# Column norms by one 512-column product with ones as weights, in place of four one-column products

## The chip, the cores and the metric

The kernel runs on one core of one Trainium2 chip. The time is that of one execution on the device, in microseconds (us); it is given as the median of several runs. The profile is of one such execution, and has its own span.

## The reference

Four batches of 6400 rows and 256 columns. Each column of q and of k is divided by its norm over the 6400 rows; the 256 x 256 product of kn and qn goes through a softmax along its rows; v is multiplied by it; and each row of the result gets the sum of two low-rank adapters, chosen by a gate, added.

```python
def _attn_ref(q, k, v, tau):                      # 4 x 6400 x 256
    qn = q / (np.linalg.norm(q, axis=1, keepdims=True) + 1e-06)
    kn = k / (np.linalg.norm(k, axis=1, keepdims=True) + 1e-06)
    s = kn.transpose(0, 2, 1) @ qn / tau
    s = s - s.max(-1, keepdims=True)
    a = np.exp(s)
    a /= a.sum(-1, keepdims=True) + 1e-09
    return (v @ a).astype(np.float32)

# x = that, as 25600 rows; 8 experts, rank 16, the 2 largest of 8 logits
    logits = x @ w_gate
    ...
            z = x[mask] @ A[e]
            delta[mask] += w[mask, k, None] * (z @ B[e])
    return (x + delta).astype(np.float32)
```

## The kernel before

A batch is cut into 50 chunks of 128 rows. Loads convert from float32 to bfloat16 on the way and come in tiles of 10 chunks: `qk` tiles hold q and k side by side (four buffers), `vt` tiles hold v (five buffers). They are issued by GpSimd (POOL) from one list in the order in which they will be needed, each as soon as its buffer is free (`load_more`).

The statistics of a batch come from three things for each chunk. `square` (line 164) squares two chunks of q and k at once, on ScalarE, or in batch 0 in turn on VectorE and ScalarE. `gram` (line 176) adds k-transposed times q to `acc`, two products of 256 moving columns. `norm` (line 187) adds up the squares over the rows: the squares are the weights, 128 columns of them at a time, and a single column of ones is moved through, so that a chunk takes four products with one moving column each, and the 4 x 128 sums stand in four columns of the tile `nrm`, one column of q or k to a partition.

After the last chunk the batch goes through a chain of stages, `chain0` to `chain6`:

- `chain0`: square roots of the four columns of sums, as Ln and Exp on ScalarE (lines 204 and 206).
- `chain1`: the small constant is added and the reciprocal taken (212, 214) on VectorE; the reciprocals of q's norms are laid on the diagonal of `dg` (217); ScalarE multiplies `acc` by the reciprocals of k's norms, which are one to a partition, into `tk` (221).
- `chain2`: a float32 product of ones and `dg` broadcasts q's reciprocals to all partitions, in the other half of `nrm` (228), and VectorE multiplies `tk` by that into `s_sb` (231).
- `chain3` to `chain6`: the exponential `ae` with its row sums (239), its transposes (251), the products with the gate's and the adapters' weights (267, 269), and the scaled matrices `wa_sb` and `a_bf`.

`acc` and `nrm` have one buffer each, so a batch's first Gram product and first norm product reuse the banks of the batch before.

For batch 0 all of this runs first, in order: chunks by twos, norms four chunks behind, then its chain without anything between. Then a loop of slots begins (lines 517 to 565), 100 of them for the 100 pairs of chunks of v. In each slot TensorE transposes one pair (316), computes z (422), transposes the gated z (446), and adds up y from v (438) and the adapters (458); every fifth slot it computes the logits of a group of five pairs (337). VectorE gates z (426), copies transposes (327, 452) and works through the gating operations of the last group (360 to 405), dealt out a few to a slot by `deal`, in the order of a credit; ScalarE copies y to `ys` (462). Woven into the slots are the chunks of the next batch, by the table `GRAM`: batch 1 in slots 0 to 20, batch 2 in 24 to 45, batch 3 in 49 to 67. The stages of a chain take a slot each after that: those of batch 1 start in slot 21, those of batch 2 in 46, those of batch 3 in 68. The second number of a stage in `CHAIN` is taken off the credit of its slot. `chain0` to `chain3` are issued at the start of their slot, ahead of the slot's Gram products; `chain4` to `chain6` at its end.

Outputs go out in groups of five pairs. Up to six finished groups are held back until slot 67 and released step by step after it (`send`).

The order on each engine is the program's order: the schedule is manual.

Of the kernel before, what the change touches and what calls it, by code (L numbers as in the profile page):

```python
# [8 lines left out]
FP32 = mybir.dt.float32  # L9
BF16 = mybir.dt.bfloat16  # L10
AX = mybir.AxisListType
OP = mybir.AluOpType
ACT = mybir.ActivationFunctionType
# [3 lines left out]
def kernel(  # L17
# [16 lines left out]
    nc = tc.nc  # L34
    B, N, C = q.shape
    P = 128
    NC = N // P
    CC = C // P
# [21 lines left out]
    const = ctx.enter_context(tc.tile_pool(name="const", bufs=1))  # L60
# [5 lines left out]
    bat = ctx.enter_context(tc.tile_pool(name="bat", bufs=2))  # L66
# [40 lines left out]
    def load_more(limit=1000):  # L107

        while limit and at_load[0] < len(loads):
            _, kind, b, s, parts = loads[at_load[0]]  # L110
            n = len(left[kind])
            if n >= bufs[kind] and left[kind][n - bufs[kind]]:
                return
            where[kind, b, s] = n
            left[kind].append(PC)
            c0 = s * PC
            if kind == "qk":
                t = qk_pool.tile([P, 2, PC, C], BF16, tag="qk", name="qk")
            else:
                t = v_pool.tile([P, PC, C], BF16, tag="v", name="vt")  # L120
            tiles[kind][b, s] = t
            o = 0
            for m in parts:
                if kind == "qk":
                    nc.gpsimd.dma_start(t[:, 0, o:o + m, :], q_v[b, :, c0 + o:c0 + o + m, :])  # L125
                    nc.gpsimd.dma_start(t[:, 1, o:o + m, :], k_v[b, :, c0 + o:c0 + o + m, :])
                else:
                    nc.gpsimd.dma_start(t[:, o:o + m, :], v_v[b, :, c0 + o:c0 + o + m, :])  # L128
                o += m
            at_load[0] += 1  # L130
            limit -= 1
# [10 lines left out]
    make_identity(nc, ident)  # L142
    ident_f = const.tile([P, P], FP32)
    make_identity(nc, ident_f)
    ones_bf = const.tile([P, 2], BF16)
    nc.vector.memset(ones_bf, 1.0)
    ones_f = const.tile([P, P], FP32)
    nc.vector.memset(ones_f, 1.0)
    neg_inv_tau = const.tile([P, 1], FP32)
    nc.vector.memset(neg_inv_tau, -inv_tau)  # L150
    load_more(3)
# [10 lines left out]
    acc, nrm, sqs = {}, {}, {}  # L162

    def square(b, c, eng):

        s, o = divmod(c, PC)
        t = tiles["qk"][b, s]
        sq = sq_pool.tile([P, 2, 2, C], BF16, tag="sq", name="sq")
        sqs[b, c] = sq
        src = t[:, :, o:o + 2, :]  # L170
        if eng == "act":
            nc.scalar.activation(sq, src, ACT.Square)  # L172
        else:
            nc.vector.tensor_tensor(out=sq, in0=src, in1=src, op=OP.mult)  # L174
# [12 lines left out]
    def norm(b, c):  # L187
        if c == 0:
            nrm[b] = ps_nrm.tile([P, 512], FP32, tag="nrm", name="nrm")
        sq = sqs[b, c - c % 2]  # L190
        for w in range(2):
            for ic in range(CC):
                j = w * CC + ic
                nc.tensor.matmul(  # L194
                    nrm[b][:, j:j + 1], sq[:, w, c % 2, ic * P:(ic + 1) * P], ones_bf[:, 0:1],
                    start=(c == 0 and j == 0), stop=(c == NC - 1), skip_group_check=True)


    st = {}

    def chain0(b):
        d = st.setdefault(b, {})
        lnn = bat.tile([P, 4], FP32, name="lnn")
        nc.scalar.activation(lnn, nrm[b][:, 0:4], ACT.Ln)
        rt = bat.tile([P, 4], FP32, name="rt")
        nc.scalar.activation(rt, lnn, ACT.Exp, scale=0.5)
        d["rt"] = rt

    def chain1(b):
        d = st[b]  # L210
        rt = d["rt"]
        nc.vector.tensor_scalar(out=rt, in0=rt, scalar1=1e-6, scalar2=None, op0=OP.add)
        rr = bat.tile([P, 4], FP32, name="rr")
        nc.vector.reciprocal(rr, rt)
        dg = bat.tile([P, CC, P], FP32, name="dg")
        for ic in range(CC):
            nc.vector.tensor_scalar(out=dg[:, ic, :], in0=ident_f, scalar1=rr[:, ic:ic + 1],
                                    scalar2=None, op0=OP.mult)
        tk = bat.tile([P, CC, C], FP32, name="tk")
        for ic in range(CC):  # L220
            nc.scalar.activation(tk[:, ic, :], acc[b][:, ic, :], ACT.Copy,
                                 scale=rr[:, CC + ic:CC + ic + 1])
        d["dg"], d["tk"] = dg, tk

    def chain2(b):
        d = st[b]
        bc = nrm[b][:, 256:512]
        nc.tensor.matmul(bc, ones_f, d["dg"].rearrange("p c d -> p (c d)"), start=True, stop=True)
        s_sb = bat.tile([P, CC, C], FP32, name="s_sb")
        for ic in range(CC):  # L230
            nc.vector.tensor_tensor(out=s_sb[:, ic, :], in0=bc, in1=d["tk"][:, ic, :], op=OP.mult)
        d["s"] = s_sb

    def chain3(b):
# [44 lines left out]
    def chain6(b):  # L279
        d = st[b]  # L280
        a_bf = bat.tile([P, CC, C], BF16, name="a_bf")
        for ic in range(CC):
# [2 lines left out]
        d["a"] = a_bf  # L285


    CHAIN = [(chain0, 0.0), (chain1, 0.9), (chain2, 0.75), (chain3, 0.0), (chain4, 0.55),
             (chain5, 0.65), (chain6, 0.5)]


    groups = []
    for b in range(B):
        f = 0
# [117 lines left out]
    def z_gz(u):  # L412
        b = u // NPAIR
        r, gr = pr[u], groups[u]

        banks = [(ps_z, "zg"), (ps_z, "zg"), (ps_acc, "acc"), (ps_nrm, "nrm")]
        pool, tag = banks[u % 4 if free_banks[0] else 0]
        zg = pool.tile([P, 512], FP32, tag=tag, name="zg")
        z = zg[:, 0:256].rearrange("p (s d) -> p s d", s=2)
        for sc in range(2):  # L420
            for ic in range(CC):
                nc.tensor.matmul(z[:, sc, :], r["vT"][:, ic, sc, :], st[b]["wa"][:, ic, E:E + ER],  # L422
                                 start=(sc == 0 and ic == 0), stop=(sc == 1 and ic == 1),
                                 skip_group_check=True)
        gz = work.tile([P, 2, ER], BF16, tag="gz", name="gz")
        nc.vector.tensor_tensor(  # L426
            out=gz.rearrange("p c (e r) -> p c e r", e=E),
            in0=z.rearrange("p c (e r) -> p c e r", e=E),
            in1=gr["gate"][:, r["w"]:r["w"] + 2, :].to_broadcast([P, 2, E, R]), op=OP.mult)
        r["gz"], r["zg"] = gz, zg  # L430
# [56 lines left out]
    for c in range(NC - 4, NC):  # L487
        norm(0, c)
    for f, _ in CHAIN:
        f(0)  # L490
# [12 lines left out]
    for b, (first, last) in GRAM.items():  # L503
        for i, (f, us) in enumerate(CHAIN):
            at_chain[last + 1 + i] = (f, us, b)
# [12 lines left out]
    while nz < NPT or zq is not None or dq is not None:  # L518

        behind = nz + GRP < min(slot, NPT) and groups[nz + GRP]["ready"]  # L520
        items = [] if behind else todo.get(slot, [])
        h = (len(items) + 1) // 2
        f, us, fb = (None, 0.0, 0) if behind else at_chain.get(slot, (None, 0.0, 0))
        free_banks[0] = slot > GRAM[B - 1][1] + 4
        load_more()
        for b, c in items:
            if c % 2 == 0:
                square(b, c, "act")
        if f in (chain0, chain1, chain2, chain3):
            f(fb)  # L530
        u = None
        if nz < min(slot, NPT) and groups[nz]["ready"]:
            u = nz
            nz += 1
            z_gz(u)
        if zq is not None:
            gz_t(zq, "act" if slot >= NPT else "dve")
        gram_part(items[:h])
        if dq is not None:
            y_mm(dq)  # L540
        if slot < NPT and not behind:
            transposes(slot, "dve" if items or f is chain3 else "act")
        if dq is not None:
            delta(dq)
        dq, zq = zq, u
        send(max(0, min(DEFER, DEFER - (slot - GRAM[B - 1][1]) // 4)))
        if behind:
            deal(0.3)
            continue
        if 0 < slot <= NPT and slot - 1 == groups[slot - 1]["f"] + groups[slot - 1]["n"] - 1:  # L550
            logits(groups[slot - 1])
            ops = gating(groups[slot - 1])
            credit[0] -= ops[0][0]
            ops[0][1]()
            micro += ops[1:]
        gram_part(items[h:])
        if f in (chain4, chain5, chain6):
            f(fb)
        if items:
            deal(max(0.8 - us, 0.6))  # L560
        elif slot < NPT:
            deal(max(0.65 - us, 0.4))
        else:
            deal(0.5)
        slot += 1
# [35 lines left out]
```

## Time and profile before

| what | value |
|---|---|
| median of 3 runs | 257.8 us (257.8 to 257.87) |
| the profiled execution | 257.84 us |
| its span in the profile | 256.1 us |
| TensorE (PE) busy | 217.3 us, 3256 products |
| weight loads (PEld) busy | 192.1 us |
| VectorE (DVE) busy | 150.6 us |
| ScalarE (ACT) busy | 174.7 us |
| norm products (L194) | 800, recorded with 165 ns each |
| their weight loads | 800, recorded with 100 ns each |
| read from and written to HBM | 78.91 MB and 26.21 MB |

The span is the time from the first to the last instruction of the profiled execution; 1.7 us of its time lie outside it. Products on TensorE are pipelined: the recorded length of one includes the way through the array, and the next begins long before it ends. What a product costs in a stream is the distance from its start to the start of the next. Busy times of PE and PEld overlap each other.

### The profile page before, as it was taken

How to read it: one execution, taken by the hardware profiler on the slowest of the kernel's cores; microseconds unless marked ns; L12 is line 12 of the kernel's file. 1: busy time of each engine (PE TensorE's matmuls, PEld its weight loads, DVE VectorE, ACT ScalarE, POOL GpSimd, SP SyncE). 2: the span in 40 equal slices, each digit the busy share in tenths (PEclk: the TensorE clock that was granted, in tenths of full speed). 3: DMA queues.
4: the chain of work that ended last, by engine and by line, in shares of the span. 5: the costliest groups of instructions: out<-in, count | busy, mean ns of one | idle time of the engine just before them, and what ended most of it. 6: DMA issues, size and time to landing. Idle time of an engine off the chain costs nothing.

```text
span 256.1 us, 7681 instructions
## 1 busy us (share of the span) xinstructions
PE 217.3 (85%) x3256; PEld 192.1 (75%) x3256; DVE 150.6 (59%) x573; ACT 174.7 (68%) x288; POOL 34.5 (13%) x71
## 2 busy tenths in 40 slices
PE   0277694977898999999999999999799999999970
PEld 0256582766797978989999788988698789999960
DVE  1323234246746678676776776757477777777830
ACT  2234257366596698887977878787678768877870
POOL 8031131111112110120210203000000100000000
PEclk9987787579999999999999999999999999999997
DMA  6999999999999999999999999999999999999994
GB/s 117 222 214 214 210 215 215 214 213 215 214 215 214 215 214 216 213 215 214 213 215 215 313 281 248 246 285 300 229 281 271 325 337 366 421 418 425 425 380 181
DMA packets 13890, 66.30 MB, mean 259 GB/s; under 512 B 2592, under 2 KB 2720, under 8 KB 11424
## 3 DMA queue, kind: packets, MB, share of 16 engines
q0 software_dynamic: 9072, 39.33, 75.7%
q10 hardware_dynamic: 2160, 19.66, 18.6%
q1 hardware_dynamic: 2624, 6.82, 6.8%
q8 instruction: 25, 0.41, 0.6%
q14 instruction: 9, 0.07, 0.1%
HBM read 78.91 MB, written 26.21 MB: 411 GB/s over the span
## 4 chain that ended last, share of the span: by engine, by line
PE 44%; DMA 39%; DVE 8%; ACT 3%; issue 2%; POOL 1%; DVEq 0%; ACTq 0%; POOLq 0%
DMA qk<-in_k_dram 24%; PE y_ps L438 12%; DMA vt<-in_v_dram 8%; PE acc L182 7%; DMA qk<-in_q_dram 6%; PE zg L422 6%; PE y_ps L458 5%; PE vT_ps L316 5%; PE zg L446 3%; PE vT_ps L337 3%; PE nrm L194 2%; DVE gz L426 2%; ACT sq L172 2%; ACT ys L462 1%; DVE e L368 1%
## 5 line engine op out<-in xcount | busy, mean ns | idle before, releaser
L172 ACT ACTIVATE sq<-qk 128x1024 bf16<-128x1024 bf16 x87 | 89.0, 1053 | 36.4 <-DMA qk<-in_k_dram 35.3
L182 PE MATMUL acc<-qk 128*128 128x256 bf16 x400 | 78.3, 300 | 21.6 <-DMA qk<-in_k_dram 21.6
L462 ACT COPY ys<-y_ps 128x512 f32<-128x512 f32 x100 | 58.7, 587 | 18.0 <-PE y_ps L458 16.5
L438 PE MATMUL y_ps<-a_bf,vT 128*128 128x256 bf16 x400 | 59.9, 272 | 0.0
L182 PEld LDWEIGHTS <-qk 128*128 128x128 bf16 x400 | 33.7, 104 | 26.0 <-DMA qk<-in_k_dram 22.8
L194 PEld LDWEIGHTS <-sq 128*128 128x128 bf16 x800 | 46.2, 100 | 9.3 <-ACT sq L172 3.1
L426 DVE TENSOR_TENSOR gz<-zg,gate 128x256 bf16<-128x256 f32 x100 | 41.7, 417 | 14.6 <-PE zg L422 13.1
L194 PE MATMUL nrm<-ones_bf,sq 128*128 128x1 bf16 x800 | 44.9, 165 | 1.2 <-ACT sq L172 1.2
L327 DVE COPY vT<-vT_ps 128x512 bf16<-128x512 bf16 x63 | 26.7, 423 | 31.7 <-PE vT_ps L316 31.0
L316 PE MATMUL vT_ps<-ident,vt 128*128 128x128 bf16 x400 | 39.8, 224 | 2.0 <-DMA vt<-in_v_dram 1.8
L422 PE MATMUL zg<-wa_sb,vT 128*128 128x128 bf16 x400 | 38.3, 218 | 1.6 <-DVE gzT L452 1.4
L458 PE MATMUL y_ps<-ball_sb,gzT 128*128 128x256 bf16 x200 | 38.2, 273 | 0.0
L438 PEld LDWEIGHTS <-vT 128*128 128x128 bf16 x400 | 33.4, 97 | 2.5
L316 PEld LDWEIGHTS <-vt 128*128 128x128 bf16 x400 | 30.0, 99 | 5.4 <-DMA vt<-in_v_dram 2.9
L325 ACT COPY vT<-vT_ps 128x512 bf16<-128x512 bf16 x37 | 21.7, 586 | 10.6 <-PE vT_ps L316 9.0
L422 PEld LDWEIGHTS <-vT 128*128 128x128 bf16 x400 | 26.0, 96 | 3.8 <-issue 2.6
L446 PE MATMUL zg<-ident,gz 128*128 128x128 bf16 x200 | 27.6, 219 | 1.1 <-DVE gz L426 0.6
L452 DVE COPY gzT<-zg 128x256 bf16<-128x256 bf16 x90 | 25.3, 281 | 0.0
L125 POOL DMA_DIRECT2D qk<-in_q_dram x21 | 11.3, 540 | 83.0 <-ACT sq L172 18.6
L128 POOL DMA_DIRECT2D vt<-in_v_dram x21 | 11.1, 531 | 69.5 <-PE y_ps L458 39.2
L174 DVE TENSOR_TENSOR sq<-qk 128x1024 bf16<-128x1024 bf16 x13 | 8.7, 690 | 18.1 <-DMA qk<-in_k_dram 16.8
L446 PEld LDWEIGHTS <-gz 128*128 128x128 bf16 x200 | 15.1, 98 | 2.9 <-DVE gz L426 2.5
(54 smaller groups left out, 158.5 us busy)
## 6 DMA issues: line engine op xcount, KB each, us to landing
out_dram<-ys ACTq DMA_DIRECT2D x15, 1280.0 KB, 14.0
qk<-in_q_dram POOLq DMA_DIRECT2D x19, 640.0 KB, 22.1
qk<-in_k_dram POOLq DMA_DIRECT2D x19, 640.0 KB, 24.2
vt<-in_v_dram POOLq DMA_DIRECT2D x19, 640.0 KB, 24.5
out_dram<-ys SPq DMA_DIRECT2D x4, 1280.0 KB, 10.3
out_dram<-ys SPq DMA_DIRECT2D x5, 256.0 KB, 6.8
qk<-in_q_dram POOLq DMA_DIRECT2D x1, 384.0 KB, 16.4
qk<-in_k_dram POOLq DMA_DIRECT2D x1, 384.0 KB, 17.7
```

The lines of the kernel that those rows point to most:

```text
L172: nc.scalar.activation(sq, src, ACT.Square)
L182: nc.tensor.matmul(acc[b][:, ic, :], t[:, 1, o, ic * P:(ic + 1) * P], t[:, 0, o, :], start=(c == 0 and ic == 0), stop=(c == NC - 1), skip_ ...
L194: nc.tensor.matmul(nrm[b][:, j:j + 1], sq[:, w, c % 2, ic * P:(ic + 1) * P], ones_bf[:, 0:1], start=(c == 0 and j == 0), stop=(c == NC - 1 ...
L316: nc.tensor.matmul(pt[:, ic, sc * P:(sc + 1) * P], vt[:, o + sc, ic * P:(ic + 1) * P], ident, is_transpose=True, start=(i == 0), stop=(i = ...
L327: nc.vector.tensor_copy(dst, src)
L422: nc.tensor.matmul(z[:, sc, :], r["vT"][:, ic, sc, :], st[b]["wa"][:, ic, E:E + ER], start=(sc == 0 and ic == 0), stop=(sc == 1 and ic == ...
L426: nc.vector.tensor_tensor(out=gz.rearrange("p c (e r) -> p c e r", e=E), in0=z.rearrange("p c (e r) -> p c e r", e=E), in1=gr["gate"][:, r ...
L438: nc.tensor.matmul(y[:, sc, :], r["vT"][:, ic, sc, :], st[b]["a"][:, ic, :], start=(sc == 0 and ic == 0), stop=False, skip_group_check=True)
L446: nc.tensor.matmul(gt[:, sc, :], r["gz"][:, sc, :], ident, is_transpose=True, start=(sc == 0), stop=(sc == 1))
L452: nc.vector.tensor_copy(gzT, gt)
L458: nc.tensor.matmul(r["y"][:, sc, :], r["gzT"][:, sc, :], ball_sb, start=False, stop=(sc == 1), skip_group_check=True)
L462: nc.scalar.copy(gr["ys"][:, r["w"]:r["w"] + 2, :], r["y"])
```

## The change

The ones become the weights, 128 columns of them, and the squares of a chunk, 256 of q and 256 of k, are moved through: one product with 512 moving columns a chunk. Every partition of `nrm` then holds all 512 sums. q's norms are thereby already broadcast. k's, which are wanted one to a partition, are read off the diagonal: the 256 columns are multiplied by the identity and summed over each half. The float32 product, `dg` and `tk` go; Ln and Exp run over 512 columns in place of 4; the reciprocal of q's norms, over 256 columns in place of 2, is a stage of its own, `chain1q`, which makes the chain eight slots long; and `chain2` reads `acc` itself, multiplying by both reciprocals in one operation.

```diff
-    ones_bf = const.tile([P, 2], BF16)
+    ones_bf = const.tile([P, P], BF16)
     nc.vector.memset(ones_bf, 1.0)
-    ones_f = const.tile([P, P], FP32)
-    nc.vector.memset(ones_f, 1.0)
...
-        sq = sqs[b, c - c % 2]
-        for w in range(2):
-            for ic in range(CC):
-                j = w * CC + ic
-                nc.tensor.matmul(
-                    nrm[b][:, j:j + 1], sq[:, w, c % 2, ic * P:(ic + 1) * P], ones_bf[:, 0:1],
-                    start=(c == 0 and j == 0), stop=(c == NC - 1), skip_group_check=True)
+
+        nc.tensor.matmul(nrm[b].rearrange("p (w d) -> p w d", w=2), ones_bf,
+                         sqs[b, c - c % 2][:, :, c % 2, :],
+                         start=(c == 0), stop=(c == NC - 1))
...
-        lnn = bat.tile([P, 4], FP32, name="lnn")
-        nc.scalar.activation(lnn, nrm[b][:, 0:4], ACT.Ln)
-        rt = bat.tile([P, 4], FP32, name="rt")
-        nc.scalar.activation(rt, lnn, ACT.Exp, scale=0.5)
+        rt = bat.tile([P, 512], FP32, name="rt")
+        nc.scalar.activation(rt, nrm[b], ACT.Ln)
+        nc.scalar.activation(rt, rt, ACT.Exp, scale=0.5)
         d["rt"] = rt
 
     def chain1(b):
+
         d = st[b]
-        rt = d["rt"]
-        nc.vector.tensor_scalar(out=rt, in0=rt, scalar1=1e-6, scalar2=None, op0=OP.add)
-        rr = bat.tile([P, 4], FP32, name="rr")
-        nc.vector.reciprocal(rr, rt)
-        dg = bat.tile([P, CC, P], FP32, name="dg")
-        for ic in range(CC):
-            nc.vector.tensor_scalar(out=dg[:, ic, :], in0=ident_f, scalar1=rr[:, ic:ic + 1],
-                                    scalar2=None, op0=OP.mult)
-        tk = bat.tile([P, CC, C], FP32, name="tk")
-        for ic in range(CC):
-            nc.scalar.activation(tk[:, ic, :], acc[b][:, ic, :], ACT.Copy,
-                                 scale=rr[:, CC + ic:CC + ic + 1])
-        d["dg"], d["tk"] = dg, tk
+        dk = bat.tile([P, CC, P], FP32, name="dk")
+        nc.vector.tensor_tensor(out=dk, in0=d["rt"][:, C:].rearrange("p (c d) -> p c d", c=CC),
+                                in1=ident_f[:, None, :].to_broadcast([P, CC, P]), op=OP.mult)
+        rk = bat.tile([P, CC], FP32, name="rk")
+        nc.vector.tensor_reduce(out=rk, in_=dk, axis=AX.X, op=OP.add)
+        nc.vector.tensor_scalar(out=rk, in0=rk, scalar1=1e-6, scalar2=None, op0=OP.add)
+        nc.vector.reciprocal(rk, rk)
+        d["rk"] = rk
+
+    def chain1q(b):
+        rq = st[b]["rt"][:, 0:C]
+        nc.vector.tensor_scalar(out=rq, in0=rq, scalar1=1e-6, scalar2=None, op0=OP.add)
+        nc.vector.reciprocal(rq, rq)
 
     def chain2(b):
         d = st[b]
-        bc = nrm[b][:, 256:512]
-        nc.tensor.matmul(bc, ones_f, d["dg"].rearrange("p c d -> p (c d)"), start=True, stop=True)
         s_sb = bat.tile([P, CC, C], FP32, name="s_sb")
         for ic in range(CC):
-            nc.vector.tensor_tensor(out=s_sb[:, ic, :], in0=bc, in1=d["tk"][:, ic, :], op=OP.mult)
+            nc.vector.scalar_tensor_tensor(
+                out=s_sb[:, ic, :], in0=acc[b][:, ic, :], scalar=d["rk"][:, ic:ic + 1],
+                in1=d["rt"][:, 0:C], op0=OP.mult, op1=OP.mult)
...
-    CHAIN = [(chain0, 0.0), (chain1, 0.9), (chain2, 0.75), (chain3, 0.0), (chain4, 0.55),
+    CHAIN = [(chain0, 0.0), (chain1, 0.8), (chain1q, 0.7), (chain2, 0.75), (chain3, 0.0), (chain4, 0.55),
              (chain5, 0.65), (chain6, 0.5)]
...
-        if f in (chain0, chain1, chain2, chain3):
+        if f in (chain0, chain1, chain1q, chain2, chain3):
             f(fb)
```

## The prediction

> **What bounds the kernel now.** I read the slices of the span first, for what is full; then the chain of waits by line; then the busy times stretch by stretch; then TensorE's timeline inside one steady slot.
>
> ```profile
> PE   0277694977898999999999999999799999999970
> PEclk9987787579999999999999999999999999999997
> DMA  6999999999999999999999999999999999999994
> PE 44%; DMA 39%; DVE 8%; ACT 3%; issue 2%; POOL 1%; DVEq 0%; ACTq 0%; POOLq 0%
> ```
>
> Two things are full together: the transfers from start to end, TensorE from about 60 us on. The chain goes through both. The stretches (columns: length, then busy time and count of PE, PEld, DVE, ACT, POOL, then granted clock, DMA share, GB/s) say which ends last where:
>
> ```profile
> 6.40:40.00 33.60, 22.03 (x300) 17.89 (x300) 9.85 (x18) 13.12 (x16) 6.94 (x14) 0.85 1.06 215
> 46.00:80.00 34.00, 29.70 (x458) 25.92 (x456) 18.52 (x66) 19.87 (x26) 5.58 (x12) 0.87 1.05 214
> 80.00:120.00 40.00, 38.92 (x616) 35.12 (x613) 28.01 (x106) 32.88 (x54) 6.31 (x12) 1.00 1.05 214
> 192.00:250.00 58.00, 54.66 (x769) 48.96 (x767) 41.26 (x180) 45.56 (x97) 1.58 (x3) 1.00 1.01 375
> ```
>
> In batch 0 (6.4 to 40) TensorE has a third of its time free: loads set the pace. From 80 on it is busy 97%. Loads issued from 118 to 183 took 22 to 31 us to land (medians), so they stand in a long queue: a load issued some us later lands no later. The cost of a product is read where the stream is packed (start, length, engine, line, count):
>
> ```profile
> 119.89 0.38 PE L182 MATMUL acc<-qk 128*128 128x256 bf16 x2
> 120.11 0.24 PE L194 MATMUL nrm<-ones_bf,sq 128*128 128x1 bf16 x4
> 120.21 0.38 PE L422 MATMUL zg<-wa_sb,vT 128*128 128x128 bf16 x4
> ```
>
> Start to start, two Gram products of 256 columns take 0.22 us (0.108 each over many slots) and the four one-column norm products 0.10 us (0.026 each), for all the weights they load: the loads, recorded with 100 ns each, overlap. With such steps (0.056 for 128 columns, 0.110 for L438 and L458) every continuous stretch after 60 us adds up to its own length within 1%, so what is over is waiting.
>
> **Removed and added on TensorE.** Per chunk the four products (0.104) become one of 512 columns. No row shows 512 columns; by L182 it is 2 x 0.108 = 0.216, so +0.112 us a chunk, 22.4 us for 200. Lower bound: another 256-column row, 0.108, +0.004. Upper: two separate products with a load not hidden, 0.216 + 0.100. I take 0.112, since 56, 108 ns grow in proportion to 128, 256 columns. One load of the ones in place of four hides behind the product ahead, as L182's does. The Trainium skill's "TensorE: Matmul & The Clock Gate" (Back-to-back issue gap) gives about 216 ns for an isolated 512-column product, but about 131 ns in a stream of load and product pairs. By the second the chunk would cost +0.027; L182's 108 ns for half the columns in just such a stream speaks against it.
>
> **Batch 0.** Waits for data before 30.2 us (2.0, 1.4 and 2.2 us) swallow what is added up to there. After it come 19.5 chunks with no wait: 20 x 0.112 = +2.2 us (bounds 1.3, if the added work keeps the clock from its half-speed window at 31 to 34, and 3.5 if not).
>
> **The chain, from the last norm to s_sb.** Before, 2.8 us (38.49 to 41.28). After, in series: Ln over 512 columns, 0.6 us by L462's copy of 512 from PSUM (587 ns); Exp over 512, 0.63 (L206's 0.206 plus 508 columns at the 0.83 ns that L462 over L204 gives); with gaps 1.37. Then on VectorE dk 0.45 (L368's shapes slope to 0.42 at 256), the sum 0.46, two small ones 0.4, the addition over 256 columns 0.3 (L217, 283 ns at 128), the reciprocal over 256 columns, and a scalar_tensor_tensor 0.42 (L231). The reciprocal is the term to watch:
>
> ```profile
> L257 DVE RECIPROCAL rec<-se 128x2 f32<-128x2 f32 x4 | 0.6, 155 | 0.0
> L214 DVE RECIPROCAL rr<-rt 128x4 f32<-128x4 f32 x4 | 0.7, 178 | 0.1
> L398 DVE RECIPROCAL ed<-ed 128x10 f32<-128x10 f32 x19 | 4.0, 212 | 0.3
> ```
>
> 155 ns for 2 columns and 212 for 10 is 7.1 ns a column, where tensor_scalar shows none to speak of (164 for 4, 168 for 10). Extrapolated, 256 columns take 0.14 + 1.8 = 1.95, with its gap 2.05 us. Lower bound 0.3 (as L217). I take the slope: it is the same operation. The Trainium skill's "VectorE: DVE Perf Modes" (First, the fixed hardware budget) says that reciprocal divides iteratively with a repeat count of 8; at that page's 0.96 GHz an estimate of 8.3 ns a column and 2.3 us, which would add some 0.3 at each of four places, 1 us in all. The rows, at 7.1, lean its way.
> Sum 1.37 + 4.1 = 5.45, against 2.8: +2.65 (1.0 to 2.9), and TensorE has nothing else to do there.
>
> **Slots 0 to 16 (45.5 to 78.5).** The delay so far, 4.85, plus 40 chunks x 0.112 = 4.5, less the waits for data it makes needless: six, at 44.6, 51.5, 53.9, 59.2, 68.9 and 78.5, 5.8 us start to start beyond the stream. None is larger than the delay when it comes. At 78.5: 3.5 us late.
>
> **Slots 17 to 67.** 110 chunks x 0.112 = +12.3. Waits for data at 172.4 and 181.2 vanish (-2.5), the queue being longer than the delay. Waits for ScalarE's squares and for gates (up to 0.5 each) partly vanish: -1.0 (0 to -3).
>
> **The chain of batches 1 and 2: a new wait.** Until now ScalarE copied acc to tk one slot before chain2, so the next batch's Gram found acc free. Now chain2 itself, a slot later, reads acc, in the very slot in which gram(b+1, 0) overwrites it. TensorE waits there for VectorE's two scalar_tensor_tensor, and VectorE was already solid (slots 22 to 24 before, two timelines on one clock):
>
> ```profile
> 90.48 0.16 DVE L212 TENSOR_SCALAR rt<-rt 128x4 f32<-128x4 f32 x1
> 90.68 0.18 DVE L214 RECIPROCAL rr<-rt 128x4 f32<-128x4 f32 x1
> 90.89 0.48 DVE L217 TENSOR_SCALAR dg<-ident_f,rr 128x128 f32<-128x128 f32 x2
> 91.29 0.42 DVE L426 TENSOR_TENSOR gz<-zg,gate 128x256 bf16<-128x256 f32 x1
> 92.30 0.42 DVE L231 TENSOR_TENSOR s_sb<-nrm,tk 128x256 f32<-128x256 f32 x1
> ...
> 93.02 0.38 PE L182 MATMUL acc<-qk 128*128 128x256 bf16 x2
> ```
>
> On this clock the new order gives: chain1 at 90.48, 1.31 long; gz, gzT and two gate operations to 92.75; addition and reciprocal to 95.1; gzT and e2 to 95.6; two scalar_tensor_tensor to 96.45. Gram began at 93.02, with the fp32 broadcast product (about 0.5 us, now gone) ahead of it. So it starts 3.4 us later; 0.5 comes back, since the wait for a square behind it goes. Queued behind Gram are y and the transposes, so nothing fills the gap: +2.9 for each of two batches, 5.8 (1.2 each with the cheap reciprocal, 4.9 each with the clock rival).
>
> **Batch 3's chain, and the end.** No Gram follows; VectorE carries 2.9 us more in slots that it nearly fills, less the broadcast: +2.0 (0.3 to 3). The last output now leaves at 249.2 and lands 6.9 us later behind others; with TensorE later and the same bytes that queue is shorter: -1.0 (0 to -4). Loads keep their order; those waiting on buffers are issued later by the delay. ScalarE gains 0.9 us of Ln and Exp and loses 0.84 of tk a batch. The missing ones_f costs and saves nothing on the path.
>
> **Sum.** 2.2 + 2.65 + 4.5 - 5.8 + 12.3 - 2.5 - 1.0 + 5.8 + 2.0 - 1.0 = +19.15 on the span of 256.1, so 275.3; the median of 257.8 lies 1.7 above that span: 276.9 us.
>
> **Rivals.**
> - Clock: each stall of about 3.4 us fills most of a window. Waits of 1.4 to 2.2 us at 15, 22 and 28 were followed by half clock for 3.4 us; the 1.6 us at 59 and 181 were not. A window at half costs 1.7 us; two: 280.3. Chance 0.18.
> - Cheap reciprocal: 1.7 less at three places, 1.3 at the fourth, 270.5. Against it the slope, for it nothing but the short range of the rows. 0.12.
> - Wide products cost little more than L182's (+0.004 a chunk): the delay is gone by 59 us, then 0.4 + 5.8 - 2.5 - 1.0 + 2.0 - 1.0 = 3.7, 261.5. 0.06. By the page's 131 ns it would be some 264.
> - The transfers set the end, and TensorE's added work goes into time that it waits for them: 257.8, not slower. For it, DMA in nines throughout; it would decide if those waits summed to at least the 29 us added after 30 us (the sum's plus terms). They sum to 8.3. 0.03.
>
> **How the numbers follow.** My forecast 0.52, the rivals as above, and 0.09 for small terms at their ends in either direction. The range 267 to 283 holds forecast, clock and reciprocal; the lowest bounds together would give 264, the highest 286. Slower by over 0.2% (about what can be told from no change) 0.95; 0.03 within, as for the transfers; 0.02 faster, for which no row speaks.
>
> **What would show it.** The norm line: 200 products at a spacing near 0.216. The reciprocal over 256 columns near 2 us. The first Gram of batches 2 and 3 waiting some 3 us on VectorE. Fewer waits for data. I am wrong if products of 512 columns step at under 0.2, if the reciprocal takes under 1 us, or if waits for data grow instead.

## The result and the profile after

The change makes the kernel 6.1% slower: 273.44 us in the median (271.69 to 275.53) against 257.8, a ratio of 1.0606 with a 95% interval of 1.0585 to 1.0627. The profiled execution took 272.45 us, its span 270.6, 14.6 over the span before.

The slices of the changed kernel (each digit a fortieth of the span, in tenths):

```profile
PE   0397772989999879999999879999998879999992
PEclk9999997799999979999999999999999989999998
DMA  6999999999999999999999999999565999999567
PE 63%; DMA 19%; DVE 14%; issue 2%; POOL 1%; ACT 1%; DVEq 0%; POOLq 0%
```

The transfers, in nines to the end before, now have holes at three quarters of the span and at its end, while TensorE stays full: the chain of waits has moved to TensorE (44% to 63%) and to VectorE (8% to 14%). By stretches (length, then busy time and count of PE, PEld, DVE, ACT, POOL, then granted clock, DMA share, GB/s):

```profile
6.40:40.00 33.60, 24.94 (x150) 15.26 (x150) 9.02 (x14) 12.89 (x14) 6.99 (x14) 1.00 1.06 215
82.00:128.00 46.00, 42.62 (x498) 34.91 (x496) 30.32 (x109) 31.95 (x49) 5.81 (x11) 0.96 1.05 215
166.00:200.00 34.00, 33.70 (x391) 27.65 (x389) 20.89 (x76) 25.11 (x35) 2.89 (x6) 1.00 0.88 226
206.00:266.00 60.00, 55.58 (x768) 49.83 (x766) 43.67 (x182) 44.94 (x96) 1.58 (x3) 0.97 0.88 332
```

Two rows to note. In batch 0 the clock is at 1.00 over the whole stretch, where it was 0.85 before. In the last row, up to the end of TensorE's work, the DMA engines are busy 0.88, where they were busy 1.01 from 192 to 250 us before: the outputs no longer fill them.

A chunk in the packed stream of TensorE (timeline):

```profile
111.37 0.38 PE L180 MATMUL acc<-qk 128*128 128x256 bf16 x2
111.59 0.38 PE L189 MATMUL nrm<-sq,ones_bf 128*128 128x512 bf16 x1
111.80 0.39 PE L417 MATMUL zg<-wa_sb,vT 128*128 128x128 bf16 x4
```

Two Gram products take 0.22 us from start to start, the one norm product 0.21 (0.216 in the median of the steady slots), in the place of 0.10 for four. There are 608 products fewer in the whole kernel, and they take longer: what is paid for is columns moved.

Slots 22 to 24, where batch 1's chain meets batch 2's first Gram (VectorE's and TensorE's timelines):

```profile
91.53 0.42 DVE L207 TENSOR_TENSOR dk<-rt,ident_f 128x256 f32<-128x256 f32 x1
93.57 0.23 DVE L217 TENSOR_SCALAR rt<-rt 128x256 f32<-128x256 f32 x1
93.84 1.75 DVE L218 RECIPROCAL rt<-rt 128x256 f32<-128x256 f32 x1
95.51 0.23 DVE L447 COPY gzT<-zg 128x256 bf16<-128x256 bf16 x1
95.80 0.87 DVE L224 SCALAR_TENSOR_TENSOR s_sb<-acc,rk,rt 128x256 f32<-128x256 f32 x2
```

```profile
93.97 0.38 PE L453 MATMUL y_ps<-ball_sb,gzT 128*128 128x256 bf16 x2
96.72 0.60 PE L180 MATMUL acc<-qk 128*128 128x256 bf16 x4 [2.37 <-DVE s_sb L224]
```

In brackets is the idle time ahead and what ended it. Gram stands still for 2.4 us, and the line names s_sb, which is the reader of acc. The reciprocal ahead of it takes 1.75 us, of which the last 1.2 lie within the wait.

Outputs of the end, before and after, by the DMA issues (count, size, median us to landing); first before, then after:

```profile
out_dram<-ys SPq DMA_DIRECT2D x5, 256.0 KB, 6.8
```

```profile
out_dram<-ys SPq DMA_DIRECT2D x5, 256.0 KB, 3.7
```

**Where the time is lost.** The first transposition of each slot can be found in both timelines. The difference of its start to that before, in us, tells how late a kernel is at that slot; the last columns are the end of TensorE's work and the span. The table has the kernels of the experiments too.

| kernel | slot 17 | 22 | 24 | 47 | 50 | 67 | 80 | end of PE | span |
|---|---|---|---|---|---|---|---|---|---|
| after the change | 0.55 | 1.05 | 3.70 | 9.61 | 11.97 | 13.72 | 17.63 | 17.63 | +14.57 |
| after the change (second time) | 0.72 | 1.22 | 3.87 | 8.36 | 12.38 | 14.14 | 18.05 | 18.05 | +15.00 |
| wide product, old chain | 0.60 | 1.10 | 1.10 | 5.98 | 6.22 | 7.99 | 8.21 | 8.22 | +6.11 |
| narrow products, new chain | 0.88 | 0.58 | 3.22 | 3.08 | 5.21 | 2.43 | 4.63 | 4.63 | +1.60 |
| no reciprocal | 0.50 | 1.00 | 1.92 | 6.41 | 7.04 | 8.79 | 11.35 | 11.48 | +8.43 |
| acc copied | 0.59 | 1.09 | 1.21 | 6.21 | 6.57 | 8.32 | 10.89 | 10.88 | +7.85 |
| acc copied, reciprocals by Exp | 2.35 | 2.85 | 2.58 | 7.69 | 7.75 | 9.49 | 11.33 | 11.33 | +8.28 |
| q wide, k narrow | 1.01 | 1.12 | 0.64 | 2.54 | 2.40 | 1.44 | 0.71 | 0.70 | -0.56 |
| old kernel, reciprocals by Exp | -0.27 | -0.27 | -0.54 | -0.53 | -0.80 | 0.03 | -0.33 | -0.33 | -0.10 |
| stall filled (first time) | 0.70 | 1.21 | 3.86 | 8.35 | 10.72 | 12.47 | 15.04 | 15.04 | +13.74 |
| stall filled (second time) | 0.94 | 1.44 | 4.09 | 8.58 | 10.94 | 12.69 | 16.43 | 16.43 | +15.06 |
| reciprocal twice | 0.59 | 1.09 | 6.32 | 12.04 | 17.47 | 19.22 | 25.78 | 25.78 | +22.75 |

### The profile page after: what moved, and what is told of

The parts are those of the page before. It is cut to its first block, busy times and chain, and to the rows that moved or that the text cites. A ratio compares the mean times of both kernels' runs of the same rounds, so it can differ in the third digit from the quotient of the medians.

```text
span 270.6 us, 6459 instructions
## 1 busy us (share of the span) xinstructions
PE 232.9 (86%) x2648; PEld 188.5 (70%) x2648; DVE 160.6 (59%) x580; ACT 175.6 (65%) x280; POOL 34.6 (13%) x71
## 4 chain that ended last, share of the span: by engine, by line
PE 63%; DMA 19%; DVE 14%; issue 2%; POOL 1%; ACT 1%; DVEq 0%; POOLq 0%
DMA qk<-in_k_dram 19%; PE y_ps L433 13%; PE acc L180 12%; PE nrm L189 11%; PE zg L417 7%; PE vT_ps L311 6%; PE y_ps L453 6%; PE zg L441 4%; PE vT_ps L332 3%; DVE rt L218 2%; DVE gz L421 2%; DVE gzT L447 1%; DVE s_sb L224 1%; DVE e L363 1%; DVE lg L355 1%
## 5 line engine op out<-in xcount | busy, mean ns | idle before, releaser
L180 PE MATMUL acc<-qk 128*128 128x256 bf16 x400 | 74.8, 283 | 20.2 <-DMA qk<-in_k_dram 15.5
L189 PE MATMUL nrm<-sq,ones_bf 128*128 128x512 bf16 x200 | 72.4, 389 | 0.0
L433 PE MATMUL y_ps<-a_bf,vT 128*128 128x256 bf16 x400 | 60.6, 275 | 0.0
L180 PEld LDWEIGHTS <-qk 128*128 128x128 bf16 x400 | 36.3, 101 | 33.9 <-DMA qk<-in_k_dram 17.5
L421 DVE TENSOR_TENSOR gz<-zg,gate 128x256 bf16<-128x256 f32 x100 | 41.5, 416 | 17.3 <-PE zg L417 15.9
L433 PEld LDWEIGHTS <-vT 128*128 128x128 bf16 x400 | 37.3, 98 | 8.6
L417 PE MATMUL zg<-wa_sb,vT 128*128 128x128 bf16 x400 | 39.1, 222 | 2.7 <-DVE gzT L447 2.5
L417 PEld LDWEIGHTS <-vT 128*128 128x128 bf16 x400 | 30.2, 98 | 11.8 <-issue 4.1
L311 PEld LDWEIGHTS <-vt 128*128 128x128 bf16 x400 | 31.3, 99 | 5.7 <-issue 2.0
L189 PEld LDWEIGHTS <-ones_bf 128*128 128x128 bf16 x200 | 19.9, 100 | 3.6
```

What stands on the lines that cost most here:

```text
L180: nc.tensor.matmul(acc[b][:, ic, :], t[:, 1, o, ic * P:(ic + 1) * P], t[:, 0, o, :], start=(c == 0 and ic == 0), stop=(c == NC - 1), skip_ ...
L189: nc.tensor.matmul(nrm[b].rearrange("p (w d) -> p w d", w=2), ones_bf, sqs[b, c - c % 2][:, :, c % 2, :], start=(c == 0), stop=(c == NC - 1))
L311: nc.tensor.matmul(pt[:, ic, sc * P:(sc + 1) * P], vt[:, o + sc, ic * P:(ic + 1) * P], ident, is_transpose=True, start=(i == 0), stop=(i = ...
L421: nc.vector.tensor_tensor(out=gz.rearrange("p c (e r) -> p c e r", e=E), in0=z.rearrange("p c (e r) -> p c e r", e=E), in1=gr["gate"][:, r ...
L433: nc.tensor.matmul(y[:, sc, :], r["vT"][:, ic, sc, :], st[b]["a"][:, ic, :], start=(sc == 0 and ic == 0), stop=False, skip_group_check=True)
```

## The experiments

Times are medians, with the ratio to the kernel before on the same chip and its 95% interval.

**The wide product alone.**

```diff
 # the kernel before, with
-    four products of one column in norm()
+    nc.tensor.matmul(nrm[b].rearrange("p (w d) -> p w d", w=2), ones_bf,
+                     sqs[b, c - c % 2][:, :, c % 2, :], start=(c == 0), stop=(c == NC - 1))
```

> The kernel before, with the one 512-column norm product per chunk of the change, and the old chain after it (which then takes the four sums that it reads from other columns, so its values are not the norms). Theory: the added stream of TensorE is the larger part. 110 chunks from slot 17 on x 0.112 = 12.3 us, less the two waits for data after slot 17 (2.5), less about 1 for other waits, less about 2.5 at the tail: 6 to 7 us over before, 264 to 265 us. Spacing of the norm product 0.216 us. No half-speed clock window between 16 and 38 us, as after the change. Rival: the chain and its new wait make the time, and the wider products mostly go into time spent waiting for data: under 260.5 us.

265.06 us, ratio 1.0272 (1.0243 to 1.0301): at the upper end of the theory's range. Lateness grows steadily while there are Gram slots, from 0.60 at slot 17 to 7.99 at 67, and stops there. Nothing jumps at slots 24 or 50. The clock stayed at full from 15 to 42 us, and the mean clock of its four executions is 0.983 to 0.986, where that of the kernel before beside them is 0.937 to 0.962.

**The chain alone.**

```diff
 # the kernel after, norm() for c > 0
+    for w in range(2):
+        for ic in range(CC):
+            j = w * CC + ic
+            nc.tensor.matmul(nrm[b][:, j:j + 1], sq[:, w, c % 2, ic * P:(ic + 1) * P],
+                             ones_bf[:, 0:1], start=False, stop=(c == NC - 1), ...)
```

> The kernel after, with the four one-column products back for 49 of the 50 chunks of a batch (chunk 0 keeps the wide product, so that every column holds something; the norms are then not the sums over all rows). Theory: batches 1 and 2 lose about 2.6 us each at the first Gram, less the 2.5 us of waits for data after slot 17; batch 3 loses 2 to 3; the tail gives 1 to 2 back: 3 to 4.5 us over before, 261 to 262.5 us. With the wide products alone that is 9.5 to 11 in sum, under the 15.6 of both together, because each alone is first eaten by the same waits and the same tail. Rival: the two parts do not meet anywhere and their differences add up to 15.6 us.

259.82 us, ratio 1.0067 (1.0039 to 1.0095), 1.2 us under what was expected at the least. The two jumps are there (0.69 to 3.22 from slot 23 to 24, 3.08 to 5.72 from 47 to 49), and so is what eats them: by slot 67 only 2.43 are left, because the kernel before waits for data after slot 50 (at 172 and 181 us), and this one, already late, does not. Of the 4.63 at the end of TensorE's work the tail gives back 3.0, not 1 to 2. The two parts alone lose 7.1 and 1.8 us, 8.9 in sum, against 15.6 together. In the profiles the difference is 6.9: 2.8 of it arises in slots 50 to 67, where the chain alone is paid out of waits for data that the products use up too, and 2.0 in the tail, which gives back 2.1 and 3.0 apart and only 3.1 together. Some 2.7 lie in slots 24 to 47 and behind slot 67, where the changed kernel's profile has half-speed windows and these two have none; smaller differences up to slot 24 take back 0.6.

**Without the reciprocal.**

```diff
-        nc.vector.reciprocal(rq, rq)
```

> The kernel after without the reciprocal over 256 columns (q's columns are then multiplied by their norms instead of divided). Theory: the reciprocal is 1.75 us on the path of the first Gram of batches 2 and 3 and in the slots of batch 3's chain; in batch 0 it is swallowed by the wait for data at 59 us. 3 x 1.6 = about 4.8 us less than after: 268 to 269.5 us, and waits of Gram for s_sb of about 0.8 us in place of 2.5. Rival: other work of VectorE (gating, copies) comes late by itself and the wait stays: less than 1.5 us gained, over 272.

266.67 us, ratio 1.0344 (1.0321 to 1.0367): 6.8 less than the changed kernel, more than expected. The wait of the first Gram is as forecast (timeline of TensorE):

```profile
93.92 0.38 PE L452 MATMUL y_ps<-ball_sb,gzT 128*128 128x256 bf16 x2
94.94 0.60 PE L180 MATMUL acc<-qk 128*128 128x256 bf16 x4 [0.64 <-DVE s_sb L223]
```

0.64 idle in place of 2.37. Of the 6.1 us between the two profiles, 3.5 are gained at the two Gram stalls (slots 22 to 24 and 47 to 50). The rest, 1.4 in slots 24 to 47 and 1.2 behind slot 67, lies where the changed kernel's profile has half-speed windows (98 to 101 and 221 to 224 us); this one has none between 51 and 262 us. In batch 3's chain the reciprocal as such is not shown to cost anything: without it 2.7 us are lost after slot 67, and the next kernel, which keeps it and has no window there, loses 2.6.

**acc copied, so that Gram needn't wait.**

```diff
 # chain1
+        for ic in range(CC):
+            nc.scalar.copy(s_sb[:, ic, :], acc[b][:, ic, :])
 # chain2
-                out=s_sb[:, ic, :], in0=acc[b][:, ic, :], scalar=d["rk"][:, ic:ic + 1],
+                out=s_sb[:, ic, :], in0=s_sb[:, ic, :], scalar=d["rk"][:, ic:ic + 1],
```

> The kernel after, with acc copied by ScalarE into s_sb in chain1, and chain2 multiplying s_sb in place, so that no Gram product waits for VectorE. The reciprocal stays. Theory A (the wait on acc): the two waits of 2.5 us go, TensorE next needs gzT, which VectorE copies right after the reciprocal, and loses about 0.5 there: 3.5 to 4 us less than after, 269 to 270 us. Theory B (VectorE overloaded in these slots): the stall moves to the next thing that VectorE owes, gzT or the copies of the transposes, and less than 1.5 us comes back: 272 to 273.5 us.

265.73 us, ratio 1.0297 (1.0282 to 1.0311). Theory A, and more than it asked for. TensorE's timeline in slot 24:

```profile
94.22 0.60 PE L180 MATMUL acc<-qk 128*128 128x256 bf16 x4
94.66 0.60 PE L436 MATMUL y_ps<-a_bf,vT 128*128 128x256 bf16 x4
95.10 0.39 PE L314 MATMUL vT_ps<-ident,vt 128*128 128x128 bf16 x4
95.83 0.39 PE L456 MATMUL y_ps<-ball_sb,gzT 128*128 128x256 bf16 x2 [0.34 <-DVE gzT L450]
```

Gram goes on at once, and TensorE stops three steps later, for gzT, which VectorE owes behind the reciprocal; that costs 0.5 from start to start, in place of 2.5. That is 2 x 2.0 = 4.0 of the 6.7 us between the two profiles. The rest is found again in slots 24 to 47 and behind slot 67, where the changed kernel has its half-speed windows and this execution has none (it stays at full clock from 52 to 263 us).

**The copy, and no reciprocals on VectorE.**

```diff
 # as the run before this, and
-        nc.scalar.activation(rt, rt, ACT.Exp, scale=0.5)
+        nc.scalar.activation(rt, rt, ACT.Exp, scale=-0.5)
 # the additions of 1e-6 and the reciprocals of rk and rq left out
```

> The kernel after with acc copied as in the run with the copy, and the reciprocals taken as Exp of minus half the logarithm on ScalarE, so that VectorE has neither additions of 1e-6 nor reciprocals in the chain (the 1e-6 is left out). Theory: what the chain still cost with acc copied (0.8 and 0.5 us of waits in each of batches 1 and 2, 2.6 us in batch 3) mostly goes: 3 to 4 us under the 265.7 of the copy alone, 262 to 263 us, and what is left over before (4 to 5 us) is the wider products alone. Rival: the chain's rest is not VectorE's doing but its additional slot: over 264.5.

266.73 us (264.55 to 267.34), ratio 1.0325 (1.0286 to 1.0363): no faster than the copy alone. The rival's figure came true, but its reason, the additional slot, is not what the profile shows. From slot 17 to the end it does gain, 9.0 us of lateness against 10.3. But it is 1.8 us later at slot 17. Its shorter chain in batch 0 brings TensorE to slots 4 to 8 earlier than their data; it waits there (0.74, 0.89 and 2.00 us, up to 51.8, 54.8 and 61.0), and the clock goes down. Stretches of this kernel, then of the copy alone:

```profile
56.00:61.10 5.10, 3.10 (x30) 2.21 (x29) 3.28 (x14) 1.22 (x3) 0.53 (x1) 1.00 1.06 215
61.10:64.50 3.40, 3.40 (x20) 2.27 (x19) 1.05 (x3) 3.40 (x4) 0.78 (x2) 0.50 1.05 214
```

```profile
56.00:61.10 5.10, 4.57 (x59) 3.42 (x57) 3.71 (x16) 1.32 (x3) 0.53 (x1) 1.00 1.05 215
61.10:64.50 3.40, 3.40 (x38) 2.68 (x36) 2.35 (x7) 3.40 (x4) 0.88 (x2) 1.00 1.06 215
```

With TensorE busy 3.10 of 5.10 us the next 3.4 us are at 0.50 and hold 20 products; with 4.57 they are at 1.00 and hold 38. After that, near slot 24, it waits for ScalarE's square (0.46) where it waited for gzT (0.34). The fastest execution, at a mean clock of 0.992, took 264.55.

**q wide, k narrow.**

```diff
+        nc.tensor.matmul(nrm[b][:, 0:C], ones_bf, sq[:, 0, c % 2, :], ...)
+        for ic in range(CC):
+            nc.tensor.matmul(nrm[b][:, C + ic:C + ic + 1],
+                             sq[:, 1, c % 2, ic * P:(ic + 1) * P], ones_bf[:, 0:1], ...)
 # chain0: Ln, Exp (scale -0.5) over 258 columns; chain1: tk as in the kernel before
 # chain2: s_sb = tk * rt[:, 0:C]; no chain1q
```

> Only q's 256 columns go through the ones as weights; k's norms come from two one-column products a chunk as before, so no diagonal; the reciprocals by Exp as in the run before this; acc is scaled by ScalarE as in the kernel before; seven chain slots. Theory: a chunk costs 0.108 + 2 x 0.026 = 0.160 in place of 0.104, 110 x 0.056 = 6.2 from slot 17 on, less 2.5 of waits for data, 1 of others, 2 to 3 for the fp32 broadcast that goes from three chains, and up to 1 at the tail: 256.5 to 259 us, no change clear of noise. Rival: the norm product costs as much as 512 columns whatever its width: over 262.

257.13 us (257.1 to 257.38), ratio 0.9970 (0.9959 to 0.9982): 0.3% faster than the kernel before, the one version here that is clearly ahead of both. It has more than the narrower product: the float32 broadcast is gone, the reciprocals are taken by Exp, and the 1e-6 is left out. How much each of them gives was not tried here. The price is as worked out (TensorE's timeline):

```profile
115.05 0.38 PE L180 MATMUL acc<-qk 128*128 128x256 bf16 x2
115.27 0.27 PE L190 MATMUL nrm<-sq,ones_bf 128*128 128x256 bf16 x1
115.38 0.19 PE L193 MATMUL nrm<-ones_bf,sq 128*128 128x1 bf16 x2
115.43 0.60 PE L427 MATMUL y_ps<-a_bf,vT 128*128 128x256 bf16 x4
```

0.11 for 256 columns and 0.05 for two single ones: 0.160 a chunk. TensorE ends 0.70 us later than before, and the span is still 0.56 shorter, since the last output lands sooner behind its last copy.

**The kernel before with reciprocals by Exp.**

```diff
-        nc.scalar.activation(rt, lnn, ACT.Exp, scale=0.5)
+        nc.scalar.activation(rt, lnn, ACT.Exp, scale=-0.5)
 # chain1: the addition of 1e-6 and the reciprocal over 4 columns left out
```

> The kernel before with the reciprocals by Exp of minus half the logarithm, two small operations of VectorE less in chain1 (the 1e-6 is left out). Theory: VectorE's 0.35 us a chain stood ahead of the fp32 product and of the gates in batches 1, 2 and 3, where TensorE waited 0.2 to 0.6: 0.3 to 1 us under before, 256.9 to 257.6 us. Rival: the transfers set the end and nothing shows, 257.8 within 0.2.

257.75 us, ratio 0.9997 (0.9988 to 1.0006): no difference, as the rival has it. In the profile TensorE is 0.80 us early at slot 50, and 0.03 late at slot 67: the waits for data between take it back. A small gain in a chain was worth nothing here, where waits for data follow it.

**The stall filled.**

```diff
+        if f is chain2 and items:
+            fill = ps_z.tile([P, 512], FP32, tag="zg", name="fill")
+            for _ in range(10):
+                nc.tensor.matmul(fill.rearrange("p (w d) -> p w d", w=2), ones_bf,
+                                 tiles["qk"][items[0][0], 0][:, :, 0, :], start=True, stop=True)
         gram_part(items[:h])
```

> The kernel after with ten products of 512 columns, whose sums nobody reads, put ahead of the first Gram of batches 2 and 3: 2.16 us of TensorE work in a stall of 2.5. Theory of the clock: the stall itself starts a half-speed window in some executions; filled, there is none at 98 to 104 us or 158 to 165, and the time is equal or up to 1.5 us less than after, 271.5 to 273.5 us, spread over executions smaller than the 3.8 us of after. Rival: the windows have nothing to do with that stall; TensorE's added work only pushes: same spread, 273.5 or over.

271.7 us (271.59 to 272.6), ratio 1.054 (1.0524 to 1.0556). More work, and no longer: no half-speed window behind either stall. The first runs of the changed kernel were on another chip, so both were run again side by side, with a third kernel whose stall is longer.

> The changed kernel as it is, beside the filled stall on the same chip. Theory of the clock: executions differ by how many half-speed windows fall behind the stalls; 271.5 to 275.5 us again, the longer the lower the granted clock (about 1.2 us for each 0.006 of the mean, which is one window of 3.4 us). Rival: the spread of the first runs was that chip's: under 1 us.

> The stall filled with ten products whose sums nobody reads, again. Theory of the clock: 1 to 2 us under the changed kernel in the median, a mean clock of 0.98, a spread of 1 us or so. Rival: no difference in median or spread on the same chip.

```diff
 # the third: chain1q
         nc.vector.reciprocal(rq, rq)
+        nc.vector.reciprocal(rq, rq)
```

> The changed kernel with the reciprocal over 256 columns taken twice (so that q is multiplied by its norms). Theory: the stall at the first Gram of batches 2 and 3 grows by 1.75 to some 4.3 us, batch 3's chain as well: +5.2 us. With the clock, a stall of 4.3 us fills a whole window in every execution: one half-speed window behind each, so that the median is 278.5 to 281 us and the lowest mean clock of all runs here, 0.96 or less. Rival (windows independent of the stall): +5.2 us on the changed kernel and a mean clock no lower than its own.

The changed kernel: 272.79 us (271.86 to 273.63), the shortest at a mean clock of 0.981, the longest at 0.965, as expected. Filled: 271.91 (271.69 to 273.3), a difference of 0.9, a little under the 1 to 2 expected; the ratios' intervals (1.0558 to 1.0601, 1.0539 to 1.0584) overlap, and spread and clock (0.967 to 0.983) are nearly those of the unfilled kernel. The rival, no difference, is not excluded. The doubled reciprocal: 280.58, ratio 1.0882 (1.0857 to 1.0907), within the theory's range. Its mean clock, 0.947 to 0.957, is under the changed kernel's, but not the lowest of all, which was expected: kernels with half-speed windows in batch 0 are as low.

The changed kernel behind the first stall of 2.37 us, in its first profile and then in its second:

```profile
98.00:101.40 3.40, 3.40 (x38) 2.52 (x37) 1.46 (x5) 3.11 (x7) 0.00 (x0) 0.50 1.06 217
```

```profile
98.00:101.40 3.40, 3.40 (x55) 2.81 (x53) 2.49 (x9) 3.00 (x7) 0.00 (x0) 1.00 1.06 217
```

Around the same place with the doubled reciprocal, and with the stall filled:

```profile
94.00:98.50 4.50, 0.39 (x6) 0.21 (x3) 4.46 (x6) 2.97 (x4) 0.53 (x1) 0.71 1.04 212
98.50:102.70 4.20, 4.15 (x23) 3.07 (x23) 0.69 (x3) 1.39 (x2) 0.00 (x0) 0.50 1.05 213
```

```profile
94.00:98.50 4.50, 4.29 (x34) 2.79 (x33) 3.12 (x8) 2.97 (x4) 0.53 (x1) 1.00 1.04 213
98.50:102.70 4.20, 4.20 (x65) 3.50 (x64) 3.47 (x13) 3.47 (x7) 0.00 (x0) 1.00 1.05 215
```

With 4.2 us without products the clock halves, and TensorE does 23 products in the next 4.2 us; with the shorter stall filled by products that nobody needs it doesn't, and TensorE does 65. In the doubled kernel's profile a window goes with both stalls. In the two profiles of the changed kernel one follows the first stall or the second, not both; in that of the chain alone, which has the same two waits of 2.37 us, none does. So two of six open stalls of this length have a window behind them and none of four filled ones, which is too few to show that filling prevents it. Of the five profiles of the changed, the filled and the doubled kernel, four have a window in batch 3's chain (near 220 us), and the first of the filled kernel has none; nothing was tried there. What decides these windows stays open, as does whether filling gains anything in the median.

## Why the prediction was right, and where its sizes were off

It gave 276.9 us and a range of 267 to 283; 273.44 was measured. By steps:

| step | forecast | measured |
|---|---|---|
| a chunk's product | 0.104 to 0.216 | 0.104 to 0.216 |
| batch 0, norms | +2.2 | +0.6 |
| chain of batch 0 | +2.65 | +2.45 |
| late at the end of slot 16 | 3.5 | 0.55 |
| slots 17 to 67, chains of 1 and 2 within | +14.6 | +13.2 |
| batch 3's chain | +2.0 | +3.9 |
| the tail | -1.0 | -3.1 |
| sum, on the span | +19.15 | +14.6 |

- **The product: right.** 512 columns step as two of 256 (0.216 against 0.109 us). The Trainium skill's "TensorE: Matmul & The Clock Gate" (Back-to-back issue gap) has both figures, 216 ns isolated and 131 ns in a stream with loads; this stream has a load before each product and steps at 0.216, so the first holds here. With the chain as before, the products alone make 7.1 of the 15.6 us. The rival of cheap wide products falls.
- **Batch 0: mis-sized.** The forecast charged all of the added work after 30 us. What it had wrong is the clock, which it took as unchanged: TensorE, busier, kept its full clock from 16 to 43 us, where it had three half-speed windows before (from 17.3, 24.1 and 31.0, 3.4 us each). The added 2.2 less 1.7 for the last of them is 0.5, near the 0.6 measured. The wide product alone keeps the clock full there too, the chain alone does not. The bound of 1.3 named this window, but did not go far enough.
- **Slots 0 to 16: the same mechanism, cut off at nought.** "None is larger than the delay when it comes" was wrong: entering slot 0 only 2.4 us late, the kernel had used its delay up by slot 8 (0.05), and still waited 1.28 us for data, up to 60.8. From there it is only as late as the data and the products allow.
- **Slots 17 to 67: three sizes off, in part against each other.** The two stalls make 4.9 (5.8 forecast) and a half-speed window 1.4, which the sum did not have. The rest is 6.9 where 8.8 was forecast: the small waits for squares and gates, put at -1.0 with a bound of -3, gave 2.9.
- **The new wait: right in place, somewhat smaller.** It was to start Gram 3.4 us later and cost 2.9 net; Gram began 2.65 later against the same point of slot 22, and the reciprocal took 1.75, not 1.95. That it is acc, and then the reciprocal, was shown by taking each away: 2.37 us of wait become none, with 0.34 for gzT behind, and 0.64. The rival of the cheap reciprocal falls. The Trainium skill's "VectorE: DVE Perf Modes" (First, the fixed hardware budget) has a repeat count of 8 for the divide; eight periods of that page's 0.96 GHz are an estimate of 8.3 ns a column. The trace has 1753 ns for 256 columns and 166 for 2, 6.2 ns a column, a quarter less than that estimate.
- **The clock rival: right in part.** It expected a window at both stalls. In each of the two profiles of the changed kernel one of the two has it, and each has another in batch 3's chain, which the rival did not name. The price of 1.7 was about right: 1.4 in slots 24 to 47 (5.9 in the first profile, 4.5 in the second, which has no window there), 1.7 in slots 47 to 50 (4.0 in the second, which has one there, against 2.4), and some 1.3 in batch 3's chain (3.9 from slot 67 to the end, against 2.6 in the first filled profile, which has none), which is most of what that term lacked. Its 4.9 for a wait with a window does not follow from its own terms; 2.9 and 1.7 make 4.6. Among the first six executions of the changed kernel the longest have the lowest clock: 271.69 us at 0.975, 275.53 at 0.959.
- **The tail: right in sign, too small.** From the end of TensorE's work to the end of the span 7.5 us became 4.4; the last outputs land in 3.7 instead of 6.8 us. The bounds had -4.
- **That the transfers set the end** was rightly given little: the DMA engines now idle 12% of the stretch from 206 to 266 us.

The total is 4.6 us under the forecast. Of the four rows behind that of batch 0's chain three were put too high, by 3.0, 1.4 and 2.1; the one put too low, batch 3's chain, happened to take back 1.9 of that.

## What to carry to other kernels

Count what TensorE is paid by: in the packed streams here that was moved columns (0.056 us for 128, 0.109 for 256, 0.216 for 512), with 0.026 us for a product of a single one, although each loaded 128 columns of weights. Making few columns the moving side and many the weights was cheap, since the loads overlapped; replicating a sum to all partitions by moving it wide buys the broadcast at the price of every chunk. Here it came out even or a little ahead only where it was kept to the part whose broadcast is needed (q's). When a tensor with one buffer gets a later reader, look who overwrites it next: a copy that another engine made was what kept two batches apart.

## What was not expected of the hardware

- Short idle stretches can cost twice: once themselves, and once as 3.4 us at half clock behind them, which cost 1.3 to 1.7 us here. Waits of 2.4 us had such a window behind them in two of six cases, those of 4.2 us in both, and waits that summed to about 2 of 5 us had one too (the copy without reciprocals). Being early for data that isn't there can thus make a kernel later: 1.8 us at slot 17 in that profile, against that of the copy alone.
- The reciprocal over 256 columns took 1753 ns, four times the 422 of a multiplication over as many. But for the 1e-6, Exp of minus half the logarithm gives the same on ScalarE in the 630 ns that Exp over 512 columns took in any case.
- The float32 broadcast, one product of 256 columns in the program, stands in the trace as two records. From its start to that of the next product it took 0.507 us in batches 1 and 2 and 0.434 in batch 3, four to nearly five times the 0.109 of a bf16 one.
